# A fused attention and rational-MLP kernel on one core: the two banks of one PSUM tile become two tiles, and the order of operations is planned anew from chunk 2 on

## The chip, the core and the metric

The kernel runs on one core of a Trainium2 chip. The core has five engines that run side by side, each through its own list of instructions in order: TensorE (PE, matrix products, with its weight loads listed as PEld), VectorE (DVE), ScalarE (ACT), GpSimd (POOL) and SyncE (SP), which here issues all DMA transfers. An instruction that needs another engine's result waits on a semaphore, and everything behind it on its engine waits too. Matrix products land in PSUM, a memory of eight banks, each of 512 fp32 values in every one of 128 partitions; DVE and ACT read it there.

The metric is the time of one execution in microseconds (us), as the median of the runs shown.

## The reference

Eight batches of eight heads, 576 tokens, head size 64. Four heads see a window of 32 tokens back, four a dilated window (every fourth token of 128). The result, 4608 tokens of 512 features, goes through an MLP with a rational activation:

```
scores = where(mask, q @ k.T / 8, -1e9)
attn   = exp(scores - max) ; attn = attn / (sum(attn) + 1e-9) ; x = attn @ v
h = x @ w_in                                  # 4608x512 @ 512x2048
P = a0 + a1*h + a2*h^2 + a3*h^3
Q = 1 + |b0|*|h| + |b1|*h^2
y = (P / (Q + 1e-6)) @ w_out                  # 4608x2048 @ 2048x512
```

All is fp32 at the edges. A matrix product is made of three products of split numbers: high by high, high by low, low by high.

## The kernel before, in words

**Work.** The 4608 tokens are nine chunks of 512 columns (0 to 8), the 2048 hidden features sixteen tiles of 128. For chunks 0 to 6 one tile of the first product (`h<-xh,wi`) is 12 matmuls into one PSUM bank of tag `h`; the activation is a chain of some twelve ACT, DVE and POOL operations on that bank and on SBUF buffers; the second product (`out<-gh,wo` and `out<-gl,wo`) is 3 matmuls for each of four output tiles. Attention is done in 48 units, spread between the tiles of the chunks, and uses a PSUM tile of two banks, `pair`. Its probabilities are transposed by a trip through DRAM: DVE writes `u`, SP stores it (`turned<-u`) and loads it back as `pT`, and PE then does `pair<-v,pT`.

**Quads.** Chunks 7 and 8 are done together, after attention is over. Two feature tiles of both chunks form a quad (eight quads, 0 to 7): its four h tiles come from seven block products instead of eight, in a Winograd scheme, with sums of weights and of inputs that were made ahead (`sums`, `place`). A product is 6 matmuls (method `times`). A quad has four banks: x and y come from tag `h`, and z and v are the two halves of `pair`, free by then:

```
self.banks = {"z": pair[:, 0], "v": pair[:, 1]}
```

In `Quad.plan` the seven products are m1 (into x), m6 (y), m5 (z), m7 (v), then m2 added onto x, m4 onto y, m3 onto z. Between them stand u1 (ACT copies x to SBUF as `mixed`, after m1; m2 waits for it), u2 (DVE adds y to `mixed`), u3 (DVE adds `mixed` and v into y, `hy<-mixed,pair`; m4 waits for it), u4 (DVE adds z to `mixed`), c22 (DVE adds `mixed` to v, in place) and c12 (ACT writes `mixed` to z; m3 waits for it). Each finished bank goes through the activation chain: ACT reads it twice (`place<-pair`, the absolute value, and `t<-pair`), DVE multiplies `t<-t,pair`, writes the bank twice (`pair<-t,na_t,pair` and `pair<-pair,na_t,r`), and reads it for the last time in `place<-place,pair` (called g2 in the code). m5 and m7 of the next quad write the banks z and v after that reading. `place` in these rows is the SBUF buffer that holds the absolute value.

**Order.** The whole kernel is first a list of operations with engines, dependencies and a rank (class `Plan`). `Plan.run` walks through a timeline by costs written in the code and lets the ready operation of lowest rank go first; the order that it finds is pinned on every engine. Ranks are worked out from due times, and then thousands of them are overwritten by a table (`RANK`); a second table (`ONLY`) binds some operations to one engine. The planner books z and v as two buffers (`bank_z`, `bank_v`). The waits in the program are not the planner's: the tile layer below puts them in, from which tiles an instruction reads and writes, and `pair` is one tile to it.

L768 in the rows is the helper that issues every matmul, L771 ACT's, L774 and L777 DVE's, L780 POOL's, L765 the one for DMA.

Of the kernel before, what the change touches and what calls it, by code (L numbers as in the profile page):

```python
# [19 lines left out]
P = 128  # L20
# [717 lines left out]
def tile_attention_moe(  # L738
# [715 lines left out]
    def out_banks():  # L1454
        if not late_pool:
            early_banks.close()
            late_pool.append(ctx.enter_context(tc.tile_pool(name="psum_out", bufs=1, space=bass.MemoryType.PSUM)))
        return late_pool[0]

    after_att = []  # L1460

    def tail_space():
        if not after_att:
# [452 lines left out]
```

## Time and profile before

| what | value |
|---|---|
| three runs | 925.05, 922.99, 922.22 us; median 922.99 |
| the profiled execution, its own time | 924.96 us |
| its span, first to last instruction | 923.0 us |
| PE busy, whole span | 879.7 us (95%) |
| DVE, ACT, POOL busy | 786.5 (85%), 682.9 (74%), 537.0 us (58%) |
| mean granted TensorE clock | 0.99 of full speed |

The profiled execution took 1.96 us more than its span, and 1.97 us more than the median of the three runs. The span is what the rows are about. A share of the whole span averages over stages that differ: loading and attention at the start, chunks 0 to 6 with attention in between, the quads from about 730 us to 889 us, and the last output products after them.

### The profile page before, as it was taken

The page shows a single profiled execution, that of the slowest core. Times are in us where ns is not written, and L with a number is a line of the kernel's source. Part 1 is how long each engine was busy: PE and PEld are TensorE (multiplying, and loading weights), DVE is VectorE, ACT ScalarE, POOL GpSimd, SP SyncE. Part 2 cuts the span into 40 slices and gives each one's busy share as a digit, 9 for nine tenths or more (in the row PEclk, how much of TensorE's full clock was granted, in tenths as well). Part 3 has the DMA queues.
Part 4 walks back from the last instruction along what each step waited for, and adds up shares of the span by engine and source line. Part 5 has one row for each costly group of instructions (what it writes and reads, how often), then busy time and mean ns, then how long its engine had stood idle before and what let it go on. Part 6 is the DMA issues. An engine that isn't in the chain of part 4 may idle for free.

```text
span 923.0 us, 20775 instructions
## 1 busy us (share of the span) xinstructions
PE 879.7 (95%) x7994; PEld 679.3 (74%) x7994; DVE 786.5 (85%) x1396; ACT 682.9 (74%) x1097; POOL 537.0 (58%) x478
## 2 busy tenths in 40 slices
PE   5699999999999999999999999999999989989998
PEld 3344588888888888778878888787777867766776
DVE  4889999998998989888899779888988788877773
ACT  1977798877677777777877788777787787878772
POOL 1767366754556565567686456566678644444453
PEclk9789999999999999999999999999999999999999
DMA  9855841321533444335564223334540245233023
GB/s 348 299 176 153 301 167 57 122 76 67 174 117 106 133 145 133 106 113 178 157 205 139 76 82 115 107 102 132 204 138 12 81 133 177 99 93 129 32 92 136
DMA packets 93538, 124.91 MB, mean 135 GB/s; under 512 B 39552, under 2 KB 64768, under 8 KB 92928
## 3 DMA queue, kind: packets, MB, share of 16 engines
q1 hardware_dynamic: 93440, 123.60, 41.2%
q8 instruction: 62, 1.02, 0.5%
q14 instruction: 36, 0.29, 0.1%
HBM read 85.95 MB, written 37.62 MB: 134 GB/s over the span
## 4 chain that ended last, share of the span: by engine, by line
PE 60%; DVE 19%; ACT 7%; DMA 5%; POOL 4%; issue 4%; SPq 1%; DVEq 0%; POOLq 0%; ACTq 0%
PE out L768 27%; PE h L768 23%; PE pair L768 7%; ACT r L771 4%; DVE a L777 3%; DVE h L777 2%; DVE t L774 2%; DVE pair L777 2%; POOL a L780 2%; DVE place L777 1%; ACT t L771 1%; DMA qk<-in_qk_dram 1%; SPq L765 1%; PE hy L768 1%; DMA pT<-turned 1%
## 5 line engine op out<-in xcount | busy, mean ns | idle before, releaser
L768 PE MATMUL out<-gh,wo 128*128 128x512 f32 x1088 | 337.8, 392 | 0.0
L768 PE MATMUL h<-xh,wi 128*128 128x512 f32 x832 | 278.2, 395 | 5.9 <-DVE a L777 5.9
L768 PEld LDWEIGHTS out<-gh,wo 128*128 128x128 f32 x1088 | 202.4, 188 | 43.4 <-ACT gh L771 0.4
L780 POOL TENSOR_TENSOR a<-r,a 128x512 f32<-128x512 f32 x98 | 128.1, 1307 | 151.2 <-ACT r L771 142.3
L768 PE MATMUL out<-gl,wo 128*128 128x512 f32 x544 | 212.1, 390 | 0.7 <-POOL gl L780 0.7
L768 PEld LDWEIGHTS h<-xh,wi 128*128 128x128 f32 x832 | 156.1, 188 | 47.1 <-DVE a L777 12.7
L768 PE MATMUL h<-xl,wi 128*128 128x512 f32 x416 | 162.1, 390 | 0.0
L780 POOL TENSOR_TENSOR gl<-a,gh 128x512 fp32r<-128x512 f32 x94 | 129.8, 1381 | 10.8 <-ACT gh L771 10.2
L771 ACT ACTIVATE r<-a,ln_bias 128x512 f32<-128x512 f32 x112 | 81.0, 723 | 65.4 <-POOL a L780 59.5
L768 PEld LDWEIGHTS out<-gl,wo 128*128 128x128 f32 x544 | 102.1, 188 | 22.8 <-POOL gl L780 1.3
L771 ACT ACTIVATE r<-a,ab_t 128x512 f32<-128x512 f32 x112 | 91.3, 815 | 21.5 <-DVE a L777 13.3
L771 ACT ACTIVATE r<-r,exp_bias 128x512 f32<-128x512 f32 x144 | 104.1, 723 | 4.1
L777 DVE SCALAR_TENSOR_TENSOR h<-h,na_t,r 128x512 f32<-128x512 f32 x112 | 84.1, 751 | 24.5 <-ACT r L771 23.6
L777 DVE SCALAR_TENSOR_TENSOR a<-a,r 128x512 f32<-128x512 f32 x112 | 85.0, 759 | 21.6 <-ACT r L771 20.2
L771 ACT ACTIVATE t<-h,na_t 128x512 f32<-128x512 f32 x112 | 86.6, 773 | 16.9 <-PE h L768 13.8
L768 PEld LDWEIGHTS h<-xl,wi 128*128 128x128 f32 x416 | 78.2, 188 | 15.7 <-POOL xl L780 0.2
L771 ACT ACTIVATE a<-h 128x512 f32<-128x512 f32 x112 | 66.3, 592 | 27.9 <-PE h L768 25.7
L777 DVE SCALAR_TENSOR_TENSOR h<-t,na_t,h 128x512 f32<-128x512 f32 x112 | 84.1, 751 | 2.7
L774 DVE TENSOR_TENSOR t<-t,h 128x512 f32<-128x512 f32 x112 | 75.7, 676 | 6.2 <-ACT t L771 5.6
L780 POOL TENSOR_TENSOR place<-r,place 128x512 f32<-128x512 f32 x32 | 42.0, 1314 | 64.3 <-ACT r L771 64.3
L777 DVE SCALAR_TENSOR_TENSOR a<-a,h 128x512 f32<-128x512 f32 x104 | 71.1, 683 | 2.8
L771 ACT ACTIVATE gh<-a 128x512 fp32r<-128x512 f32 x93 | 58.2, 626 | 10.1 <-DVE a L777 6.5
(179 smaller groups left out, 1337.0 us busy)
## 6 DMA issues: line engine op xcount, KB each, us to landing
qk<-in_qk_dram SPq DMA_DIRECT2D x48, 448.0 KB, 4.6
v<-in_vp_dram SPq DMA_DIRECT2D x48, 384.0 KB, 4.3
out_dram<-os SPq DMA_DIRECT2D x36, 256.0 KB, 2.2
wi_raw<-in_w_in_dram SPq DMA_DIRECT2D x16, 512.0 KB, 6.2
wo_raw<-in_w_out_dram SPq DMA_DIRECT2D x16, 512.0 KB, 6.4
turned<-u SPq DMA_DIRECT2D x42, 192.0 KB, 2.1
pT<-turned SPq DMA_DIRECT2D x84, 96.0 KB, 2.6
sums<-wi SPq DMA_DIRECT2D x24, 256.0 KB, 2.8
```

The lines of the kernel that those rows point to most:

```text
L765: pin(nc.sync.dma_start(dst, src))
L768: pin(nc.tensor.matmul(o, lhs, rhs, start=start, stop=stop, skip_group_check=skip))
L771: pin(nc.scalar.activation(o, i, func, **kw))
L774: pin(nc.vector.tensor_tensor(o, x, y, op))
L777: pin(nc.vector.scalar_tensor_tensor(o, x, s, y, op0, op1))
L780: pin(nc.gpsimd.tensor_tensor(o, x, y, op))
```

## The change

Each of z and v becomes a PSUM tile of one bank, made anew for every quad (`hz_0`, `hv_0`, `hz_1` and so on) from a pool that takes the place of `pair` when the first quad needs it. `pair` itself, which attention still uses, moves into a pool of its own that is closed then. So the tile layer sees eight times two tiles where it saw the halves of one.

```diff
-    pair = psum.tile([P, 2, 512], F32, tag="pair", name="pair")
+    pair_space = ExitStack()
+    pair = pair_space.enter_context(tc.tile_pool(name="psum_pair", bufs=1, side="right", space=bass.MemoryType.PSUM)).tile([P, 2, 512], F32, name="pair")
...
+    after_pair = []
+
+    def quad_bank(tag, j):
+        if not after_pair:
+            pair_space.close()
+            after_pair.append(ctx.enter_context(tc.tile_pool(name="psum_quad", bufs=1, side="right", space=bass.MemoryType.PSUM)))
+        return after_pair[0].tile([P, 512], F32, tag=tag, name=f"h{tag}_{j}")
...
         def h(self, n):
-            self.banks[n] = h_bank(f"{n}_{self.j}")
+            self.banks[n] = h_bank(f"{n}_{self.j}") if n in ("x", "y") else quad_bank(n, self.j)
...
-            self.banks = {"z": pair[:, 0], "v": pair[:, 1]}
+            self.banks = {}
...
-                    if first and bank in ("x", "y"):
+                    if first:
                         self.h(bank)
```

The other part is the two tables. Of the some 2740 entries of `RANK` 2565 differ, all from operation 580 on, and of `ONLY` many; two lines stand for them:

```diff
-    580: 287.16723987701425, 581: 55.362085636455284, 582: -265.0247441431534, 583: 10.390660580619492, 584: -3.63423917315967, 585: 256.2901997213647,
...
+    580: -172.74332857628426, 581: 55.362085636455284, 582: -265.0247441431534, 583: 10.390660580619492, 584: 14.87888869293468,
```

The matmuls are the same 5626 in both programs, and on every engine the first stretch of the order is the same too (on PE the first 724 rows of the order's 2384, on DVE 483 of 1290). Behind it the order is new. Three places show what moved. Buffer numbers stand at the ends of names, and `hz_4` is the bank z of quad 4.

On PE, in quad 4: m7 (first operands `place1`, `place5`), m5 (`place0`, `place4`) and m4 (`place3`, `place7`), in the order of before:

```order
L768 MATMUL pair_87<-place1_8785,place8_8802 128x512 x3
L768 MATMUL pair_87<-place5_9034,place8_8802 128x512 x3
L768 MATMUL out8_1_0_9597<-gh121_9806,wo5_1059 128x512 x2
L768 MATMUL out8_1_0_9597<-gl121_9814,wo5_1059 128x512
L768 MATMUL out8_3_0_9585<-gh121_9806,wo5_1059 128x512 x2
L768 MATMUL out8_3_0_9585<-gl121_9814,wo5_1059 128x512
L768 MATMUL pair_87<-place0_8766,place19_8689 128x512 x3
L768 MATMUL pair_87<-place4_8878,place19_8689 128x512 x3
L768 MATMUL hy_4_9842<-place3_8964,place8_8802 128x512 x3
L768 MATMUL hy_4_9842<-place7_9143,place8_8802 128x512 x3
```

And the same products on PE in the order of the change:

```order
L764 MATMUL hv_4_9866<-place1_8777,place8_8811 128x512 x3
L764 MATMUL hv_4_9866<-place5_9075,place8_8811 128x512 x3
L764 MATMUL out8_1_0_9571<-gh123_9757,wo4_928 128x512 x2
L764 MATMUL out8_1_0_9571<-gl123_9771,wo4_928 128x512
L764 MATMUL hz_4_9884<-place0_8770,place19_8690 128x512 x3
L764 MATMUL hz_4_9884<-place4_8905,place19_8690 128x512 x3
L764 MATMUL out8_1_0_9571<-gh121_9797,wo5_1062 128x512 x2
L764 MATMUL out8_1_0_9571<-gl121_9801,wo5_1062 128x512
L764 MATMUL hy_4_9816<-place3_8971,place8_8811 128x512 x3
L764 MATMUL hy_4_9816<-place7_9180,place8_8811 128x512 x3
```

Between m7 and m5 stand 3 matmuls of the output instead of 6, and between m5 and m4 there are now 3 instead of none.

On DVE, at the same place: the last two readings of quad 3's banks (`place13<-place13,pair`, first v's and then z's), and u2, u3, u4, c22 of quad 4, before:

```order
L777 SCALAR_TENSOR_TENSOR place13_9279<-place13_9279,pair_87 128x512
L777 SCALAR_TENSOR_TENSOR place13_9279<-place13_9279,r127_9812 128x512
L774 TENSOR_TENSOR t128_9829<-t128_9829,hx_4_9756 128x512
L777 SCALAR_TENSOR_TENSOR pair_87<-pair_87,na_t_98,r127_9812 128x512
L777 SCALAR_TENSOR_TENSOR place13_9279<-place13_9279,pair_87 128x512
L774 TENSOR_TENSOR mixed4_9771<-mixed4_9771,hy_4_9842 128x512
L774 TENSOR_TENSOR hy_4_9842<-mixed4_9771,pair_87 128x512
L777 SCALAR_TENSOR_TENSOR hx_4_9756<-t128_9829,na_t_98,hx_4_9756 128x512
L774 TENSOR_TENSOR mixed4_9771<-mixed4_9771,pair_87 128x512
L774 TENSOR_TENSOR pair_87<-mixed4_9771,pair_87 128x512
```

And on DVE in the order of the change:

```order
L773 SCALAR_TENSOR_TENSOR place13_9289<-place13_9289,hv_3_9703 128x512
L773 SCALAR_TENSOR_TENSOR place13_9289<-place13_9289,r127_9827 128x512
L773 SCALAR_TENSOR_TENSOR hz_3_9746<-hz_3_9746,na_t_101,r127_9827 128x512
L773 SCALAR_TENSOR_TENSOR place13_9289<-place13_9289,hz_3_9746 128x512
L770 TENSOR_TENSOR hy_4_9816<-mixed4_9823,hv_4_9866 128x512
L770 TENSOR_TENSOR t128_9873<-t128_9873,hx_4_9803 128x512
L773 SCALAR_TENSOR_TENSOR hx_4_9803<-t128_9873,na_t_101,hx_4_9803 128x512
L770 TENSOR_TENSOR mixed4_9823<-mixed4_9823,hz_4_9884 128x512
L770 TENSOR_TENSOR hv_4_9866<-mixed4_9823,hv_4_9866 128x512
```

u2 has moved ahead of this stretch, and an operation on tile x that stood ahead of z's last reading now stands behind u3.

On SP, at the last attention unit, 47: the store and the load of its probabilities and the stores of quad 7's sums of weights, before:

```order
L765 DMA turned1_77<-u47_8518 128x2x192
L765 DMA left_78<-y45_8536 128x2x16
L765 DMA pT47_8567<-turned1_77 64x4x96 x2
L765 DMA sums7_86<-high7_8539 128x256 x2
L765 DMA sums7_86<-whole15_8505 128x256 x2
```

And on SP in the order of the change:

```order
L761 DMA left_78<-y45_8521 128x2x16
L761 DMA turned1_77<-u47_8549 128x2x192
L761 DMA sums7_86<-high7_8540 128x256 x2
L761 DMA pT47_8593<-turned1_77 64x4x96 x2
L761 DMA sums7_86<-whole15_8508 128x256 x2
```

The load of `pT47` has gone behind the two stores of `high7`, and the store of `u47` behind that of `y45`.

## Rows read from the trace of the kernel before

**Rows 1.** The page, part 1: busy us, share of the span, instructions.
```profile
PE 879.7 (95%) x7994; PEld 679.3 (74%) x7994; DVE 786.5 (85%) x1396; ACT 682.9 (74%) x1097; POOL 537.0 (58%) x478
```
**Rows 2.** Windows, by stretch: us, then each engine's busy us, clock, DMA.
```profile
200.00:300.00 100.00, 100.00 (x1072) 81.53 (x1072) 90.05 (x169) 70.77 (x114) 52.92 (x50) 1.00 0.38 118
...
730.00:889.00 159.00, 145.63 (x611) 112.40 (x610) 128.92 (x193) 122.38 (x194) 70.59 (x54) 1.00 0.34 113
```
**Rows 3.** Waits of PE, 730 to 889 us: us, times, longest.
```profile
PE pair L768 <- DVE t L774: 2.6, 3, 1.4
PE hx L768 <- ACT mixed L771: 1.9, 2, 1.2
PE pair L768 <- DVE place L777: 1.6, 2, 1.2
PE pair L768 <- DVE hy L774: 1.5, 1, 1.5
PE pair L768 <- ACT t L771: 1.5, 3, 0.6
PE hy L768 <- DVE hy L774: 1.4, 3, 0.9
PE pair L768 <- DVE pair L777: 1.3, 1, 1.3
PE out L768 <- POOL gl L780: 0.7, 1, 0.7
PE hy L768 <- DVE place L777: 0.2, 1, 0.2
```
**Rows 4.** Timeline, quad 2's m3: start, us, instruction, idle before.
```profile
760.82 0.60 ACT L771 ACTIVATE pair<-mixed 128x512 f32<-128x512 f32 x1 [0.54 <-DVE pair L774]
...
763.77 0.76 ACT L771 ACTIVATE t<-pair,na_t 128x512 f32<-128x512 f32 x1
...
764.58 1.65 PE L768 MATMUL pair<-place,sums_xl 128*128 128x512 f32 x6 [0.51 <-ACT t L771]
```
**Rows 5.** Timeline, quad 4's m5 and the DVE rows ahead of it.
```profile
815.70 0.69 DVE L777 SCALAR_TENSOR_TENSOR place<-place,pair 128x512 f32<-128x512 f32 x1
...
817.02 0.69 DVE L774 TENSOR_TENSOR hy<-mixed,pair 128x512 f32<-128x512 f32 x1
...
817.77 1.66 PE L768 MATMUL pair<-place,place 128*128 128x512 f32 x6 [1.54 <-DVE hy L774]
```
**Rows 6.** Timeline, quad 1's m7 and m4 and DVE around them.
```profile
750.76 0.69 DVE L777 SCALAR_TENSOR_TENSOR place<-place,pair 128x512 f32<-128x512 f32 x1 [0.88 <-ACT t L771]
...
753.21 0.69 DVE L774 TENSOR_TENSOR t<-t,pair 128x512 f32<-128x512 f32 x1 [1.16 <-PE pair L768]
...
754.72 0.70 DVE L774 TENSOR_TENSOR hy<-mixed,pair 128x512 f32<-128x512 f32 x1
```
**Rows 7.** Timeline, a product of 6 matmuls that waited for nothing.
```profile
735.89 1.52 PE L768 MATMUL hy<-place,place 128*128 128x512 f32 x6
```
**Rows 8.** Matmuls on tile hx: ns min/median/max, first and last start.
```profile
L768 PE MATMUL hx<-xh,place x32: 388/389/389, 730.4 to 854.7; 128*128 128x512 f32 x32
```
**Rows 9.** Timeline of PE: the last m3, and two output matmuls behind the quads.
```profile
887.11 1.66 PE L768 MATMUL pair<-place,sums_xl 128*128 128x512 f32 x6 [0.57 <-ACT t L771]
...
902.66 0.39 PE L768 MATMUL out<-gl,wo 128*128 128x512 f32 x1
...
910.14 0.39 PE L768 MATMUL out<-gl,wo 128*128 128x512 f32 x1
```
**Rows 10.** Waits of PE, 600 to 740 us: us, times, longest.
```profile
PE h L768 <- DVE a L777: 3.5, 7, 1.2
```
**Rows 11.** Timeline, the last attention unit's probabilities.
```profile
662.20 1.24 SPq L765 DMA_DIRECT2D pT<-turned  x2
664.22 0.81 SPq L765 DMA_DIRECT2D sums<-high  x2
...
668.13 0.72 PE L768 MATMUL pair<-v,pT 64*32 64x64 f32 x48
```
**Rows 12.** Tile pT, 640 to 670 us: from issue to landing.
```profile
DMA to landing us min/median/max: 2.5/2.6/2.7
```

More of the change, by code (lines that the diff above doesn't have):

```diff
@@ L587 @@
     183: "POOL", 185: "ACT DVE", 186: "DVE", 191: "ACT", 197: "POOL", 201: "ACT", 213: "ACT", 221: "DVE", 222: "DVE", 225: "POOL", 231: "POOL",
-    243: "ACT", 245: "POOL", 269: "POOL", 273: "ACT", 281: "ACT", 287: "ACT", 380: "POOL", 614: "POOL", 730: "POOL", 763: "POOL", 814: "DVE",
-    830: "POOL", 863: "DVE", 880: "POOL", 946: "DVE", 983: "POOL", 989: "DVE", 1021: "POOL", 1125: "DVE", 1134: "DVE", 1143: "POOL", 1179: "DVE",
-    1206: "DVE", 1233: "DVE", 1278: "DVE", 1313: "ACT", 1367: "ACT", 1404: "DVE", 1465: "ACT", 1475: "POOL", 1511: "DVE", 1861: "DVE", 1863: "DVE",
@@ L591 @@
-    2157: "ACT", 2457: "ACT", 2749: "ACT", 3049: "DVE", 3053: "DVE", 3054: "DVE", 3055: "POOL", 3058: "DVE", 3059: "ACT", 3060: "POOL", 3064: "POOL",
-    3068: "POOL", 3069: "DVE", 3070: "POOL", 3071: "POOL", 3072: "POOL", 3075: "DVE", 3079: "DVE", 3083: "POOL", 3084: "POOL", 3086: "DVE",
-    3087: "DVE", 3088: "POOL", 3089: "ACT", 3094: "POOL", 3098: "DVE", 3099: "POOL", 3102: "POOL", 3103: "POOL", 3104: "POOL", 3109: "POOL",
-    3115: "DVE", 3117: "DVE", 3118: "DVE", 3119: "ACT", 3123: "ACT", 3124: "POOL", 3128: "POOL", 3129: "DVE", 3130: "DVE", 3131: "DVE", 3132: "DVE",
@@ L595 @@
-    3135: "POOL", 3145: "POOL", 3146: "POOL", 3147: "DVE", 3148: "DVE", 3149: "ACT", 3150: "POOL", 3158: "DVE", 3161: "DVE", 3162: "POOL",
-    3163: "POOL", 3165: "DVE", 3169: "POOL", 3177: "DVE", 3178: "POOL", 3179: "DVE", 3180: "POOL", 3181: "POOL", 3182: "POOL", 3183: "DVE",
-    3187: "POOL", 3189: "DVE", 3190: "ACT", 3196: "POOL", 3198: "DVE", 3203: "ACT", 3205: "DVE", 3206: "DVE", 3207: "DVE", 3208: "POOL", 3209: "DVE",
-    3210: "DVE", 3771: "DVE", 3811: "DVE", 3817: "ACT",
+    243: "ACT", 245: "POOL", 269: "POOL", 273: "ACT", 281: "ACT", 287: "ACT", 380: "POOL", 580: "POOL", 597: "POOL", 663: "POOL", 746: "DVE",
@@ new lines @@
+    763: "POOL", 780: "POOL", 830: "DVE", 914: "DVE", 946: "DVE", 963: "POOL", 978: "DVE", 983: "POOL", 989: "DVE", 1021: "POOL", 1125: "DVE",
+    1134: "DVE", 1143: "POOL", 1179: "DVE", 1206: "DVE", 1233: "DVE", 1278: "DVE", 1313: "ACT", 1367: "ACT", 1404: "DVE", 1465: "ACT", 1475: "POOL",
+    1511: "DVE", 1861: "ACT", 1867: "ACT", 2157: "ACT", 2159: "DVE", 2453: "ACT", 2455: "DVE", 3045: "ACT", 3049: "DVE", 3054: "DVE", 3055: "POOL",
+    3056: "POOL", 3057: "POOL", 3058: "DVE", 3059: "ACT", 3060: "POOL", 3064: "POOL", 3070: "POOL", 3071: "DVE", 3072: "POOL", 3074: "ACT",
@@ new lines @@
+    3078: "ACT", 3084: "POOL", 3085: "POOL", 3086: "DVE", 3088: "POOL", 3089: "ACT", 3090: "DVE", 3093: "ACT", 3094: "POOL", 3098: "POOL",
+    3100: "POOL", 3101: "POOL", 3104: "ACT", 3105: "POOL", 3113: "POOL", 3114: "DVE", 3115: "DVE", 3116: "DVE", 3117: "DVE", 3119: "POOL", 3123: "ACT",
+    3124: "POOL", 3129: "DVE", 3130: "DVE", 3132: "DVE", 3133: "DVE", 3135: "POOL", 3138: "DVE", 3145: "POOL", 3148: "DVE", 3150: "POOL", 3158: "DVE",
+    3160: "POOL", 3161: "DVE", 3164: "ACT", 3168: "POOL", 3178: "POOL", 3179: "POOL", 3183: "DVE", 3187: "DVE", 3191: "POOL", 3195: "POOL",
@@ L599 @@
+    3196: "POOL", 3198: "DVE", 3204: "DVE", 3205: "DVE", 3206: "DVE", 3207: "DVE", 3209: "DVE", 3210: "POOL", 3813: "DVE", 3815: "ACT", 3817: "DVE",
 }
```

979 rows, old and new, of the table RANK are left out of this document.

## The prediction

> **What bounds the kernel now.** I read the page's busy times first. PE is busy for 879.7 of the span's 923.0 us, more than any other engine [rows 1], so time is lost or won where PE stands still, and an operation on another engine counts only where PE waits for it. Next I asked for windows by stage. From 200 to 300 us, with attention and chunks mixed, PE has no idle time at all, although DVE is busy for 90.05 of the 100 us; in the quads, from 730 to 889 us, PE is busy for 145.63 of 159, with DVE at 128.92 and ACT at 122.38, that is 81% and 77% [rows 2]. So the quads lose time on PE while no other engine is full: their loss is one of waiting on each other. The clock is no part of it; both windows were granted 1.00.
>
> Busy time understates this loss. A matmul's row lasts 0.39 us, but the next one starts 0.227 us after it when nothing stops it: from 902.66 to 910.14 us stand 33 matmuls, and 7.48/33 is 0.227 [rows 9]. So a pause shows as idle only beyond 0.16 us. I therefore counted matmuls in the order: from the first matmul of quad 0's m1, at 730.4 us [rows 8], to the first of quad 7's m3, at 887.11 us [rows 9], there are 600. At 0.227 us they take 136.2 us; they took 156.7. The quads lose 20.5 us, against 13.1 us that the waits view names in 17 waits [rows 3].
>
> The Trainium skill says the same in Perfetto Trace Analysis, Identifying the Most-Contended Engine: the busy share of matmuls is a poor measure of TensorE's headroom, and the busy share of weight loads a better one. By that rule the stage, at the rate of weight loads of the full window, would take 112.40/0.8153 = 137.9 of its 159 us, so 21.1 us are lost [rows 2]; by the busy time of matmuls it would be 13.4. The trace agrees with the rule, since the count of matmuls gives 20.5.
>
> **What the split removes.** The planner books z and v as two buffers, but the tile layer holds back whatever touches one half of `pair` until the last access that another engine made to either half has ended. The rows show it. In quad 2, m3 writes z. What it needs, c12, ended at 761.42 us, yet m3 starts at 764.58, right behind an ACT reading of v that began at 763.77 [rows 4]. In quad 4, m5 writes z, whose last reading (of quad 3) ended at 816.39; m5 starts at 817.77, after u3, which reads v [rows 5]. With two tiles both waits have nothing to hang on, and the order of the changed program lets m5 wait for z's own last reading alone.
>
> I sorted all 17 waits of [rows 3] in this way, by what the waiting instruction touches in the code.
> - Eight are direct: a product for one half waits for a reader or writer of the other. They are the four lines `PE pair` for DVE t, DVE hy, ACT t and DVE pair: 2.6 + 1.5 + 1.5 + 1.3 = 6.9 us in 3 + 1 + 3 + 1 waits.
> - Four are one step removed. Quad 1's m7 waits for a DVE reading of v that itself sat idle for 0.88 us behind an ACT reading of z; its m4 waits 0.9 us for u3, which stands on DVE behind a chain on z that had waited 1.16 us for m7 [rows 6]. The two other waits of hy for DVE hy have the same shape: 1.4 - 0.9 = 0.5 us. Together 0.88 + 1.4 = 2.3 us.
> - Each wait costs more than its idle time. There is the 0.16 us from above, and a product behind a wait takes 1.65 us [rows 4] where one behind none takes 1.52 [rows 7], 0.13 more. That is 0.29 us for each, 12 x 0.29 = 3.5 us.
>
> 6.9 + 2.3 + 3.5 = 12.7 us.
>
> **What comes late next.** Where one of the twelve falls, the next true condition may bind. For quad 4's m5 it is z's last reading: 816.39 us, while PE's last row ended at 817.77 - 1.54 = 816.23 [rows 5]. So 0.2 us of its 1.54 stay, and with the 0.29 about 0.5. For quad 2's m3 nothing stays. If half of the twelve keep about as much, some 6 x 0.35, 2 us come back: that share is my choice between none (0) and all of them (4). DVE and ACT must do the same work in some 10 us less: 128.92/149 is 87%, still under the 90.05% that DVE had beside a PE without idle time [rows 2].
>
> **What stays.** Five waits hang on no half: two m2 behind u1 (ACT mixed, 1.9 us), one output product behind POOL gl (0.7), one m5 behind its own bank's last reading (1.6 - 1.2 = 0.4), one m6 (0.2): 3.2 us, with 0.29 for each 4.7. The new order may cover them: in quad 4 it puts 3 output matmuls ahead of m4 where none stood, and takes 3 from between m7 and m5. But between m1 and m2 of quads 3 and 5, where both waits for u1 are, 6 matmuls stand before and after. I take nothing here; the bounds are 0 and 4.7 us of gain.
>
> **The new order in chunks 2 to 6.** The matmuls are the same 5626. PE has little to lose or win there: where it waits most, from 600 to 740 us, the largest sum is 3.5 us in seven waits for a DVE reading of h [rows 10], and a window without any idle shows that the old order was already tight [rows 2]. One place is plainly worse. Before, SP loads `pT47` from 662.20 to 663.44 us, the data are there 2.6 us after an issue [rows 12], near 666.0, and PE uses them at 668.13 [rows 11]: 2.1 us to spare. Now the load stands behind the stores of `high7`, which before were issued from 664.22 to 665.03 and had to wait for their data. Behind these, the load would end at 666.3 and land at 668.9: 0.8 us late. I take 0.5, between 0 (if `high7` comes earlier now) and 0.8. For the rest of these chunks I take 0, with 2 us to either side, less than the 3.5 us that stand there.
>
> **Sum.** -12.7 + 2.0 + 0.5 = -10.2 us. The profiled execution, 924.96 us (span 923.0 and 1.96 us around it), becomes 914.8, its span 912.8. It lies 1.97 us over the median of its three runs, so the forecast of the median is 912.8, rounded 913. A measurement tells about 0.3%, 2.8 us, from no change.
>
> **Rivals.**
> *The whole loss goes.* The new order covers the true waits too, and the 20.5 us shrink to some 4: 923.0 - 16.5 = 906.5. For it speaks that DVE at 90% leaves PE without idle time elsewhere [rows 2]; against it the two m2 with the same 6 matmuls ahead.
> *The next wait takes the place.* The activation chains of four banks share one DVE and one ACT, and the two operations ahead of a released product are often queued, not held. If only half of the 12.7 us is real, with the 0.5 it is 923.0 - 5.9 = 917. Against it: in [rows 4, 5] the product's own condition was met 3.2 and 1.4 us before it started.
> *It does nothing.* Either the waits came from the two halves only by name, or chunks 2 to 6 lose what the quads win: 922 to 924. [rows 4] speaks against the first.
> *Slower, by the trip of the probabilities through DRAM.* SP issues in order, and a `pT` load behind a store whose data are late holds the attention product on PE, and every matmul behind it. The place is each of the 32 units of chunks 2 to 6; the price is the 0.8 us of unit 47 with the 0.29 of a wait, 1.1 us. It decides from 10.2/1.1, ten such places, on; at all 32 it would be 923.0 - 10.2 + 34 = 947. Against it: only the place at unit 47 shows such a move plainly, and before 2.1 us were to spare there [rows 11].
>
> **Chances and range.** The forecast, 910 to 916: 0.57. The whole loss goes, under 910: 0.14. Half, 916 to 920.2: 0.17. Nothing, within 0.3% of 923.0: 0.07. Slower: 0.05. So faster has 0.57 + 0.14 + 0.17 = 0.88, same 0.07, slower 0.05. The range from 907 to 919.5 leaves out the lower half of the second case and the two last ones, with the upper edge of the third, under 0.2 together.
>
> **What would show it.** The first matmul on quad 0's hx should start near 730.4 us, within 2; if it is later by more, the new order costs time in chunks 2 to 6. From there to the first matmul of quad 7's m3 it should be some 146 us, not 156.7. No PE row on `hz` should wait for an ACT or DVE row on `hv`, nor the reverse, and the waits of PE in the quads should sum to some 4 us. The two m2 behind `mixed` should still wait. PE's use of `pT47` should wait for its DMA. I am wrong if the quads keep their 156 us with waits under other names, or if they shrink and the start of hx moves by as much.

## The result and the profile after

The changed kernel took 902.32 us (median of four runs, 900.63 to 903.56), the kernel before beside it 922.68: a ratio of 0.9773, interval 0.975 to 0.9797, so 20.4 us less. The forecast was 913.0 with a range of 907 to 919.5: the sign was right, the gain was twice the forecast and lay outside the range.

The page of the kernel after, its span and part 1 (busy us, share of the span, instructions), answers to [rows 1]:

```profile
span 898.8 us, 20773 instructions
...
PE 870.9 (97%) x7994; PEld 680.8 (76%) x7994; DVE 780.7 (87%) x1391; ACT 681.8 (76%) x1099; POOL 536.7 (60%) x481
```

The engines do nearly the same work in a span 24.2 us shorter. The medians differ by 20.4: this profiled execution took 900.63 us, 1.7 less than its median, and that of before about 2 more than its own.

Windows of the kernel after by stretch, in the columns of [rows 2]; most of its quads lie within 730 to 870 us, whose last 5 us are behind them:

```profile
200.00:300.00 100.00, 100.00 (x1072) 81.69 (x1072) 90.03 (x170) 71.00 (x115) 52.79 (x50) 1.00 0.37 118
...
730.00:870.00 140.00, 138.75 (x608) 113.53 (x607) 130.71 (x194) 124.12 (x198) 71.32 (x55) 1.00 0.38 125
```

PE now does in 140 us nearly what took it 159, with DVE busy for 93% of them and ACT for 89%. The waits of PE from 724 to 870 us (us, times, longest) answer to [rows 3]:

```profile
PE hy L764 <- DVE place L773: 0.8, 2, 0.4
PE hv L764 <- DVE place L773: 0.3, 1, 0.3
```

Of 17 waits and 12.7 us, three waits and 1.1 us are left. No m2 waits for u1 (`ACT mixed`) any more, and no output product for gl. The other two engines wait less as well. In the quads alone, 730 to 887 us before and 725 to 863 us after, the waits that the view names sum to 33.9 us on ACT before and 16.6 after, and to 26.6 and 8.2 on DVE. The largest line of each engine, before:

```profile
ACT place L771 <- DVE pair L777: 3.7, 4, 1.3
DVE pair L777 <- PE pair L768: 5.2, 4, 1.8
```

And after:

```profile
ACT r L767 <- POOL place L776: 5.4, 8, 1.4
DVE t L770 <- ACT t L767: 2.4, 3, 1.2
```

First and last start of the matmuls on hx, and the timeline of PE at quad 7's m3, answer to [rows 8, 9]:

```profile
L764 PE MATMUL hx<-xh,place x32: 389/389/393, 724.6 to 833.7; 128*128 128x512 f32 x32
```

```profile
863.09 1.52 PE L764 MATMUL hz<-place,sums_xl 128*128 128x512 f32 x6
```

From the first matmul on hx to the first of quad 7's m3 stand 600 matmuls, as before, and they take 138.5 us (724.6 to 863.1) instead of 156.7. At the undisturbed 0.227 us each they need 136.2. I use this stretch of 600 matmuls, counted the same way in each trace, as the measure of the quads in all that follows.

### The profile page after: what moved, and what is told of

Its sections match the earlier page's. It is cut to its first block, busy times and chain, and to the rows that moved or that the text cites. A ratio compares the mean times of both kernels' runs of the same rounds, so it can differ in the third digit from the quotient of the medians.

```text
span 898.8 us, 20773 instructions
## 1 busy us (share of the span) xinstructions
PE 870.9 (97%) x7994; PEld 680.8 (76%) x7994; DVE 780.7 (87%) x1391; ACT 681.8 (76%) x1099; POOL 536.7 (60%) x481
## 4 chain that ended last, share of the span: by engine, by line
PE 78%; DVE 10%; ACT 3%; DMA 3%; issue 3%; POOL 2%; SPq 1%; DVEq 0%; POOLq 0%; ACTq 0%
PE out L764 37%; PE h L764 28%; PE pair L764 5%; PE hz L764 2%; PE hy L764 2%; PE hx L764 2%; DVE a L773 2%; DVE h L773 2%; ACT r L767 2%; PE hv L764 1%; DVE t L770 1%; SPq L761 1%; DMA left<-y 1%; DMA qk<-in_qk_dram 1%; DVE place L773 1%
## 5 line engine op out<-in xcount | busy, mean ns | idle before, releaser
L776 POOL TENSOR_TENSOR gl<-a,gh 128x512 fp32r<-128x512 f32 x94 | 126.7, 1348 | 11.3 <-ACT gh L767 10.7
```

The source lines that it names most:

```text
L776: pin(nc.gpsimd.tensor_tensor(o, x, y, op))
```

## The experiments

Three theories stood after the result. **A**: the forecast's sum for the quads is right, and the new order brings the rest. **B**: the split alone brings it all, because ACT and DVE were held across the two halves as well, and the queues behind the held instructions carried this on into waits that name no half. **C**: the new order brings it. Of the programs this can be read beforehand: the split with before's tables has before's order on every engine, exactly, and its waits differ from before's from the quads on, on 15 instructions of PE, 32 of ACT, 44 of DVE and 3 of SP.

**The split with the old order.** The kernel after, with before's `RANK` and `ONLY`:

```diff
-    580: -172.74332857628426, 581: 55.362085636455284, 582: -265.0247441431534, 583: 10.390660580619492, 584: 14.87888869293468,
+    580: 287.16723987701425, 581: 55.362085636455284, 582: -265.0247441431534, 583: 10.390660580619492, 584: -3.63423917315967, 585: 256.2901997213647,
...
```

> The two one-bank tiles with the order of before on every engine. Theory A (the split gives what the prediction counted for it, 12.7 less 2.0 that come back, and the new order the rest): 922.7 - 10.7 = 912, within 2; PE's waits in the quads 4 to 6 us, first matmul on hx still at 730. Theory B (the split alone gives back the whole loss of the quads, the new order there nothing): 904 to 906. Theory C (the gain is the order's; the split alone changes nothing): 920 to 923.

Measured: 904.34 us (903.65 to 905.86), ratio 0.9788 [0.9769, 0.9807], 19.0 us less than before. The 600 matmuls take 138.4 us. All that is left of PE's waits there, 727 to 870 us:

```profile
PE hy L771 <- DVE place L780: 0.7, 2, 0.5
PE hv L771 <- DVE place L780: 0.3, 1, 0.3
```

B holds: A is too high by 8 us, and C is out. The waits of ACT and DVE in the quads (728 to 866 us) sum to 17.5 and 9.8 us, nearly as low as in the kernel after. Since the order is the same, the trace can be laid beside that of before instruction by instruction. Quad 2's u4 (`mixed<-mixed,pair`), c12, c22, m3 and first reading of v, then quad 3's u1 and m2, in the kernel before (start, us, instruction, idle before):

```profile
780.10 0.69 DVE L774 TENSOR_TENSOR mixed<-mixed,pair 128x512 f32<-128x512 f32 x1
780.82 0.60 ACT L771 ACTIVATE pair<-mixed 128x512 f32<-128x512 f32 x1 [0.29 <-DVE mixed L774]
781.46 0.69 DVE L774 TENSOR_TENSOR pair<-mixed,pair 128x512 f32<-128x512 f32 x1 [0.67 <-ACT pair L771]
782.21 1.66 PE L768 MATMUL pair<-place,place 128*128 128x512 f32 x6
...
783.90 0.78 ACT L771 ACTIVATE t<-pair,na_t 128x512 f32<-128x512 f32 x1 [1.93 <-PE pair L768]
...
789.26 0.58 ACT L771 ACTIVATE mixed<-hx 128x512 f32<-128x512 f32 x1
...
789.89 0.50 PE L768 MATMUL hx<-xh,sums_xh 128*128 128x512 f32 x1 [1.25 <-ACT mixed L771]
```

And the same instructions in the split with the old order:

```profile
772.64 0.69 DVE L777 TENSOR_TENSOR mixed<-mixed,hz 128x512 f32<-128x512 f32 x1
773.36 0.60 ACT L774 ACTIVATE hz<-mixed 128x512 f32<-128x512 f32 x1 [0.30 <-DVE mixed L777]
773.36 0.69 DVE L777 TENSOR_TENSOR hv<-mixed,hv 128x512 f32<-128x512 f32 x1
...
774.42 0.76 ACT L774 ACTIVATE t<-hv,na_t 128x512 f32<-128x512 f32 x1
774.48 1.52 PE L771 MATMUL hz<-place,place 128*128 128x512 f32 x6
...
779.56 0.58 ACT L774 ACTIVATE mixed<-hx 128x512 f32<-128x512 f32 x1
...
780.60 0.39 PE L771 MATMUL hx<-xh,sums_xh 128*128 128x512 f32 x1
```

Before, DVE waits 0.67 us with c22 on v until ACT has written z. Then ACT waits 1.93 us with its reading of v until m3 into z has ended: 782.21 + 1.66 = 783.87. With two tiles c12 and c22 start together at 773.36, and ACT reads v while PE writes z. u1 stands in ACT's queue behind this reading, and m2 on PE behind u1. From u4 to m2 it takes 9.8 us before and 8.0 with the split, and m2 has no idle time left. So m2's wait named u1, a tile that the split does not touch, and was caused by the halves.

The Trainium skill, in PSUM — Partial Sum Buffer, PSUM bank collisions raise a hardware error, says to guard PSUM by bank and quadrant of partitions, not by address. The trace agrees: with the waits across banks gone, ACT's reading of hv and PE's product into hz overlap from 774.48 to 775.18 us, and the product takes the undisturbed 1.52 us.

**The halves with the new order.** The kernel before, with after's tables: the tile stays whole.

```diff
-    580: 287.16723987701425, 581: 55.362085636455284, 582: -265.0247441431534, 583: 10.390660580619492, 584: -3.63423917315967, 585: 256.2901997213647,
+    580: -172.74332857628426, 581: 55.362085636455284, 582: -265.0247441431534, 583: 10.390660580619492, 584: 14.87888869293468,
...
```

> The one tile of two banks with the new order on every engine. In chunks 2 to 6 the split plays no part, so every theory expects the 5 us that the trace of the change shows there (first hx at 725). Theory A: the waits across halves stay in the quads, only the five true waits can be covered: 914 to 918. Theory B: 917 to 918, the quads as before. Theory C: 902 to 905.

Measured: 923.22 us (920.35 to 924.8), ratio 0.9989 [0.9975, 1.0002]. All three theories are 5 us or more off here. So without the split the new order gains nothing in all. The quads got 2.8 us longer (159.5 us for the 600 matmuls), and hx starts at 726.6 us, 3.8 earlier. A likely reason for the first is that the order was planned for two banks and fits halves that wait for each other worse; no run shows it.

**Half of the new order each.** Both have the split. In the first the numbers of the tables change at operation 3211, where the quads begin, from the old to the new:

```diff
-    3209: 112.28612341207533, 3210: 371.4721190023449, 3211: 102.47763173031443, 3212: -1000.5574927657149, 3213: 107.70681565124431,
+    3209: 112.28612341207533, 3210: 371.4721190023449, 3211: 104.09409635540521, 3212: 101.75009563983029, 3213: 100.0096425045279,
...
```

> The split, with the new tables for the operations of the quads and the old ones ahead of them. If chunks 2 to 6 are worth 5 us by themselves: 902.3 + 5 = 907, first hx at 730. If the two parts of the order need each other (what the middle hands over to the quads): later than 909. Theory C: 905 to 908.

The second has the new numbers up to there and the old ones from there on:

```diff
-    3210: 640.6818892514874, 3211: 104.09409635540521, 3212: 101.75009563983029, 3213: 100.0096425045279, 3214: 104.00137050192222,
+    3210: 640.6818892514874, 3211: 102.47763173031443, 3212: -1000.5574927657149, 3213: 107.70681565124431, 3214: 99.99496486634091,
...
```

> The split, with the new tables ahead of the quads and the old ones for the quads. Theory A: 912 - 5 = 907, within 2. Theory B: 900 to 902.5, the same as the whole change. Theory C (order of the quads): 915 to 918. First hx at 725 for all.

Measured: 927.5 us (ratio 1.0041 [1.0025, 1.0056]) and 929.55 (1.0066 [1.0038, 1.0095]), 23 and 25 us above the split alone. The largest of PE's waits from 718 to 905 us in the first:

```profile
PE hy L769 <- DVE place L778: 10.7, 6, 5.5
```

Its longest wait, and the window around it in the columns of [rows 2]:

```profile
774.76 2.93 PE L769 MATMUL hy<-place,place 128*128 128x512 f32 x6 [5.55 <-DVE place L778]
...
760.00:780.00 20.00, 13.68 (x47) 10.17 (x46) 13.64 (x20) 14.44 (x23) 7.65 (x6) 0.83 0.19 54
```

Behind 5.55 us without work this product took 2.93 us, and the granted clock of the window is 0.83, so a part of this run's loss is one of the clock, on top of the waits.

The forecast of the first that came true is "later than 909"; for the second all were too low by 11 us or more. The quads lost it: the 600 matmuls of the first take 161.7 us, and in the second 618 stand in that stretch and take 163.9. As an order of the quads neither was a fair test: the numbers weigh operations of both parts against each other, and in the quads PE's order follows neither plan. What they show there is that the split did not carry these two orders, which were not planned as a whole. How each order of the quads would do in its own sequence behind the other middle was not tried. Ahead of the quads it is otherwise: by the tiles that they write, the 4885 matmuls before the first on hx stand in the second run in the new order, and in the first in the old one but for 6. First start on hx is 723.6 us in the second and 727.7 in the first.

**The waits put back, engine by engine.** To the split with the old order, explicit waits are added: an instruction on hz waits for the last one of each other engine on hv, and the reverse, on the engines in `CROSS`. Tiles, banks and order stay those of the split.

```diff
+    CROSS, last_at = ("PE",), {}
+
+    def cross(i, eng, *ops):
+        bank = {n[1] for n in (getattr(getattr(x, "tensor", None), "name", "") for x in ops) if n[:3] in ("hz_", "hv_")}
+        for b in bank:
+            if eng in CROSS:
+                for (other, e), p in last_at.items():
+                    if other != b and e != eng:
+                        tc.add_manual_dep(i.ins, p.ins.name, mybir.DependencyInfo(mybir.DependencyClass.Sync, mybir.DependencyReason.DATA), reason="other half")
+            last_at[b, eng] = i
+        return i
...
-        pin(nc.tensor.matmul(o, lhs, rhs, start=start, stop=stop, skip_group_check=skip))
+        cross(pin(nc.tensor.matmul(o, lhs, rhs, start=start, stop=stop, skip_group_check=skip)), "PE", o)
...
```

On PE alone:

> Split with the order of before (904.3 in the run above); on PE alone the waits across z and v are put back, as explicit dependencies of a product on the last DVE and ACT access to the other bank. By the prediction's sum the eight direct waits cost 6.9 us and 8 x 0.29: 904.3 + 9.2 = 913.5. Queue theory (most of the loss came from ACT and DVE being held in their own queues, which made the readers late that PE waited for): 906 to 910.

On ACT and DVE, not on PE:

```diff
-    CROSS, last_at = ("PE",), {}
+    CROSS, last_at = ("ACT", "DVE"), {}
```

> The same split and order, with the waits across z and v put back on ACT and DVE alone, none on PE. By the prediction's sum only the four waits one step removed come back, 2.3 us and 4 x 0.29: 904.3 + 3.5 = 907.8, and PE's waits for u1 (ACT mixed) stay as small as without. Queue theory: 912 or more, and the waits for u1 and for POOL gl are back on PE, since what stands behind a held ACT or DVE instruction is late too.

On all three:

```diff
-    CROSS, last_at = ("PE",), {}
+    CROSS, last_at = ("PE", "ACT", "DVE"), {}
```

> The same split and order with the waits across z and v put back on all three engines. If those waits are the whole of it, and not the banks' addresses, the pool that is closed or a tile made anew: 921 to 925, as before. If some of the gain is of another kind: that much under 921.

| waits across the banks on | us (lowest to highest) | ratio to before | over the split alone | 600 matmuls, us |
|---|---|---|---|---|
| none (the split, old order) | 904.34 (903.65 to 905.86) | 0.9788 [0.9769, 0.9807] | 0 | 138.4 |
| PE | 906.97 (906.0 to 907.74) | 0.9817 [0.9799, 0.9836] | 2.6 | 141.2 |
| ACT and DVE | 914.73 (914.4 to 915.97) | 0.9903 [0.9887, 0.992] | 10.4 | 148.2 |
| all three | 923.48 (921.46 to 925.91) | 0.9995 [0.9982, 1.0007] | 19.1 | 156.3 |

With all of them the kernel is as slow as before, its 600 matmuls take what they took before, and the waits in the quads are back on each engine (12.6 us on PE, 33.5 on ACT, 26.9 on DVE): the waits across the halves are the whole of the split's effect, and the new pool and the tiles have no part in it beyond the interval, some 2 us. PE's own are worth 2.6 us, those of ACT and DVE 10.4, and 6.1 of the 19.1 appear only when both are there. The split alone was not measured beside these three; with its second measurement, 904.8 below, each is 0.5 us less. The queue theory's 906 to 910 and its 912 or more both hold; the prediction's sum had 913.5 and 907.8, the greater loss on the wrong engine. PE's waits with those of ACT and DVE put back, 718 to 900 us:

```profile
PE hx L783 <- ACT mixed L786: 2.0, 2, 1.3
PE hv L783 <- DVE place L792: 1.1, 1, 1.1
PE hy L783 <- DVE place L792: 1.0, 2, 0.6
PE hy L783 <- DVE hy L789: 0.8, 1, 0.8
PE out L783 <- POOL gl L795: 0.7, 1, 0.7
```

The two m2 behind u1 and the output product behind gl are back, with 2.0 and 0.7 us where [rows 3] has 1.9 and 0.7, although no instruction of PE was given a wait. With PE's waits alone put back, none of the three is there.

**The kernel after and the split alone, again.** Whether the order adds to the split was open: the first medians, 902.32 and 904.34, were not measured side by side, and the intervals of their ratios overlap. So both ran again on one chip. The edit from the split alone to the kernel after is the table once more:

```diff
-    580: 287.16723987701425, 581: 55.362085636455284, 582: -265.0247441431534, 583: 10.390660580619492, 584: -3.63423917315967, 585: 256.2901997213647,
+    580: -172.74332857628426, 581: 55.362085636455284, 582: -265.0247441431534, 583: 10.390660580619492, 584: 14.87888869293468,
...
```

> The kernel after, measured again beside the split in the old order, on one chip. Theory N (the new order adds to the split): 900 to 903 us, and at least 1.5 us under the split alone, the difference in chunks 2 to 6 (matmul rows 1250 to 7230 some 3 us shorter, quads the same 140.7). Theory Z (the 2 us between them was which chip and which arrival of the weights they met): within 1 us of the split alone.

> The split in the old order, again. Theory N: 903.5 to 906 us, at least 1.5 us above the kernel after. Theory Z: within 1 us of it.

Measured: 901.37 us (ratio 0.9771 [0.9747, 0.9795]) and 904.8 (0.98 [0.9782, 0.9817]), 3.4 us apart after 2.0 the first time. The ratios' intervals still overlap, so the size is loose, but both pairs agree and the traces show the place. The 600 matmuls take 138.5 and 138.3 us: the quads are the same. The difference lies ahead of them. First start on hx, in the kernel after and in the split alone:

```profile
L764 PE MATMUL hx<-xh,place x32: 388/389/390, 725.3 to 834.4; 128*128 128x512 f32 x32
```

```profile
L771 PE MATMUL hx<-xh,place x32: 388/390/393, 729.2 to 838.7; 128*128 128x512 f32 x32
```

And the largest of PE's waits from 94 to 718 us, in the same two:

```profile
PE h L764 <- DVE a L773: 2.3, 7, 0.4
```

```profile
PE h L771 <- DVE a L780: 5.5, 11, 1.2
```

In the kernel before these waits are 5.9 us, in the first pair 2.1 and 4.7. So the new order takes some 3 us of PE's waits for DVE out of chunks 2 to 6. All traces bear this out: the same 4885 matmuls stand ahead of hx in each, and it starts at 723.6 to 726.6 us in the four that have the new order there (the two above, the halves with the new order, the second mixed table) and at 727.2 to 730.4 in the seven that have the old one. Theory N, that the order adds to the split, is the likelier one.

## Why the prediction was wrong

**The loss to be won** was right. Counting matmuls gave 20.5 us lost in the quads; 18.2 of them came back (156.7 to 138.5). By weight loads, as the Trainium skill has it in Perfetto Trace Analysis, Identifying the Most-Contended Engine, the window after would need 113.53/0.8169 = 139.0 of its 140 us, with 81.69 of the full window for the rate: 1.0 lost, where the count gives 2.3 in the quads. Both say that little is left. (The lines of [rows 3] sum to 12.7 us, not to the 13.1 that I gave; the terms were taken from the lines, so nothing hangs on it.)

**What the split removes**, 12.7 us, was right in its mechanism: eleven of the twelve waits are gone, no product on hz waits at all, and products without a wait take 1.52 us. The twelfth, quad 1's m7, keeps 0.34 of its 1.2 us, for the last reading of its own bank, which is what the 0.88 in the sum had left. (The m3 of [rows 4] is quad 1's, counted from 0, and not quad 2's as I called it: quad 2's u1 starts only at 764.95 us. Nothing hangs on it.)

**What stays** is the step that failed. I sorted PE's waits by what the waiting instruction touches, and called five of them true because u1, gl and two readings of `place` hang on no half. I took nothing for them, and put the "two m2 with the same 6 matmuls ahead" against the rival that the whole loss goes. But the instruction that releases PE stands in a queue. With the order unchanged both m2 lost their waits, and they came back when ACT and DVE alone were held again. The step asked what the waiting instruction touches, and not why its releaser was late: a look at ACT's row with 1.93 us before v's reading would have answered it. Four of the five went, 3.0 us and 4.2 with 0.29 for each; quad 1's m6, 0.2 us before, still waits, 0.43 us now.

**What comes late next** failed for the same reason, with the other sign. I let 2.0 us come back, since the next condition of a freed product might bind. The next conditions were operations on ACT and DVE, and these had been held too: their waits in the quads fell from 33.9 and 26.6 us to 16.6 and 8.2. Of new waits there is one, an m6 of quad 7 with 0.33 us.

So the quads gave 18.2 where the sum had 10.7. By the view PE's waits fell by 11.6 us in 14 waits, 15.7 with 0.29 for each: 5.0 of the 7.5 us between sum and result are these, and the other 2.5 lie in pauses too short for the view. The sum's division of the gain by PE's waits was wrong as well: 6.9 us of them were direct, 9.2 with 0.29 each, but PE's waits across the banks alone cost 2.6, and those of ACT and DVE, 3.5 by the sum, cost 10.4.

**DVE's limit.** I checked DVE at 87% against the 90.05% of a full window, which was no bar. It stands at 93% in the window after, and PE still has 138.75 of 140.

**The new order** was to give 0 in chunks 2 to 6, 2 to either side, and to lose 0.5 at `pT47`. It gave 2.0 and 3.4 us in the two comparisons, for the most part from waits that [rows 10] showed: the 3.5 us for DVE's reading of h are 1.1 and 1.4 in the two traces of the kernel after. I allowed less than their size on the ground that the old order "was already tight". At `pT47` the load stands behind `high7`'s stores as expected, but the timeline after names no wait for its DMA there:

```profile
659.54 0.81 SPq L761 DMA_DIRECT2D sums<-high  x2
660.45 1.24 SPq L761 DMA_DIRECT2D pT<-turned  x2
663.71 0.56 PEld L764 LDWEIGHTS pair<-v,pT 64*32 64x32 f32 x48 [0.31 <-issue]
```

The stores now came earlier, which was the lower end of that term. Next to nothing was to spare, since the second load was issued at 661.1 us and loads land 2.4 to 2.6 us after their issue there; but the kernel before had 0.35 us of the same kind before this row, so none of the 0.31 need be a loss. The start of hx moved from 730.4 to 724.6, beyond the 2 us that I named; the split alone, in the old order, has it at 727.7 and 729.2, so 1.2 to 2.7 of that come with the execution and not with the order.

**The rivals.** "The whole loss goes", at 906.5 and with 0.14, was the right one, though for another reason than it gave: it had the new order cover the true waits, and the split took them away in the old order. It left 4 us in the quads, where 2.3 remain, and it had nothing from chunks 2 to 6. The other three did not come: little took the place of the removed waits, and no trip of the probabilities held PE up for long (PE's waits for `pT` from 94 to 718 us are 0.7 us before, 1.0 and 0.7 after). What the range left out comes to some 0.22 by the shares given, and not to "under 0.2".

## What to carry to other kernels

A wait that names a resource which the change does not touch may still come from it: before calling it independent, go from the releaser back along its own engine's queue, and read the waits of that engine too. When several engines hold each other over one shared tile, the parts do not add up (here 2.6 and 10.4 us apart, 19.1 together), so ask what is lost against the undisturbed rate as well, and do not put the likely gain far under it because single waits look independent: here 18.2 of 20.5 us came back. Two buffers that are planned as two should be two tiles: the tile layer here tracked the whole, and made accesses to one wait for the other.

## What was not expected of the hardware

DVE at 93% and ACT at 89% of a stretch beside a PE that is busy for 138.75 of 140 us: engines that take turns on four banks this full still kept PE supplied, once each wait hung on its own bank. I had taken 90% for DVE as the highest share known to go with an undisturbed PE. The trace of before had a window, from 100 to 200 us, that shows more, beside a PE that is busy for 98.75 of 100 us:

```profile
100.00:200.00 100.00, 98.75 (x728) 77.51 (x714) 94.88 (x170) 85.82 (x137) 61.24 (x55) 1.00 0.42 144
```
